# Projection of the last pairs: products 1 and 2 of the next pair issued among the last three products of a pair, in alternating PSUM banks

## Chip, cores and metric

One core of one Trainium2 chip. The metric is the device time of one execution in microseconds (us); before and after are compared by the median of several runs. The profile is of one execution, with a span that is a little shorter than its time.

## What is computed

```python
X = np.fft.rfft(x, axis=1)                    # x: 8 x 3136 x 256
y = np.fft.irfft(X * F, n=3136, axis=1)       # F: a complex filter, 1569 x 256
t = y.reshape(25088, 256)                     # tokens
h = t @ w_in                                  # 256 -> 1024
sm = softmax(h, axis=-1)
solu = h * sm
ln = (solu - mean(solu)) / np.sqrt(var(solu) + 1e-6) * g_ln
out = ln @ w_out                              # 1024 -> 256
```

## The kernel before

The Fourier filter is done as two short transforms by matrix products (49 x 64 points), one batch element after the other. Its results land in `y`, and tokens are taken from there in **blocks** of 128; there are 196 blocks, and two blocks make a **pair** (98 pairs, 0 to 97). The filter of later batch elements runs beside the token work of earlier ones; its last product (L353) and copy (L356) end at 1447.4 us of the span, and then only token work is left.

The order of all instructions on every engine is written out by hand: `step(k)` for k = 0 to 204 issues, for block k, what each engine does next, and each engine runs its own list in that order. A pair j = k // 2 takes two steps, an even and an odd one. Within a step several pairs are in flight at different depths:

- **Hidden products** (`product`, L680): `t @ w_in` of a pair of blocks is done by Strassen's scheme in Winograd's form, with seven products instead of eight. Their PSUM banks are m0 and m2 of the pool `ps_m`, and one from another pool. ScalarE keeps some copies (L690), VectorE finishes the halves of h and the row maximum (L701, L704). This is done for k < 196.
- **exp and normalizing**: two steps later ScalarE takes exp of h with a row sum (L712); VectorE makes the reciprocal of the sum (L723, L725) and solu (L728); ScalarE squares it for the variance (L730).
- **Turning**: three steps later VectorE transposes solu in 32 x 32 pieces (L738), and SyncE's queue regroups it with eight DMAs for a pair (`regroup`, L750): four write the buffer `solu_t0`, four `solu_t1`. Each of the two exists twice, so that the DMAs for pair p must wait until the last reader of pair p - 2 is done: for `solu_t1` that is product 4 of pair p - 2. For every second pair SyncE also writes and reads back the deviations (L758, L764: `rs_t`).
- **Sums for the projection** (`project_sums`, L658, GpSimd): four sums of the regrouped blocks, two in an odd step and two in the following even one.
- **Projection** (`project`, L792): `ln @ w_out` for pair p, again seven products, each of four 128 x 128 matmuls in float32, which the profile shows as 8 records. In the odd step the order is 1, 2, 6, 7, in the even step after it 5, 3, 4. Products 1, 6, 5, 3 go one after the other into one bank, 2, 7, 4 into the other; the banks are o0 and o1 of the pool `ps_o`, one each. 6, 5 and 3 are added on top of what their bank holds, 7 starts the other one anew and 4 adds to it; before each of 6, 5 and 3 ScalarE takes a scaled copy of the bank as it stands (`keep_out`, L804). VectorE finishes the four quarters of the output (`finish_out`: L811 adds a kept copy, L809 only scales). `store_out` (L819) stores the pair with two DMAs of SyncE's queue.

Nine steps lie between the first hidden product of a pair and its last projection (`LAG`). So the steps k = 196 to 204 have no hidden products any more: they project pairs 93 (second half), 94, 95, 96 and 97. This is the tail, the last 45 us of the span. In it the lists by engine are, before the change:

- TensorE: 5, 3, 4 of 93; 1, 2, 6, 7, 5, 3, 4 of 94; the same of 95, 96 and 97.
- SyncE: regroup 95 and store 93; regroup 96 first half, L758, regroup 96 second half, store 94; L764; regroup 97, store 95; store 96; store 97.
- ScalarE: with the copies of 5(93) come exp of block 194, square of 194, exp of 195, copy of 1(94), square of 195, copies of 6(94) and 5(94), and then the three copies of each pair.
- VectorE: normalizing of block 194, finish of 93, turn of 194, first finish of 94, normalizing of 195, turn of 195, and then the finishes.

The projection's first product of the next pair starts a new sum in o0, so it must wait until VectorE has read the last pair's sum there (L809); the second does the same in o1 (L811).

## Time and profile before

| what | us |
|---|---|
| median of 5 runs | 1682.4 |
| these runs, lowest and highest | 1678.14, 1689.17 |
| the profiled execution | 1687.0 |
| its span | 1685.2 |
| granted TensorE clock, mean over the span | 0.987 |

Engines: PE is TensorE (PEld its weight loads), DVE VectorE, ACT ScalarE, POOL GpSimd, SP SyncE; a q behind the name is its queue, issuing DMAs. A row of the timeline has the start, the length in us, the engine, the line of the kernel, the operation, output <- input, the number of records that were merged, and in brackets the idle time before it with the one that ended it. A row of the chain of waits has the start, the length and what the end of the kernel hung on at that time. A row of the windows has the stretch, its length, the busy us (and records) of PE, PEld, DVE, ACT and POOL, the granted TensorE clock as a share of full speed, the busy share of the DMA engines, and GB/s.

### The profile page before, as it was taken

The numbers are of one execution on the slowest core, as the hardware profiler recorded it, in microseconds if no ns is written. First come the engines' busy times: TensorE is split into PE (matmuls) and PEld (weight loads), VectorE is DVE, ScalarE is ACT, GpSimd is POOL, SyncE is SP. The second block draws the span as 40 slices with busy tenths as digits, with TensorE's granted clock in tenths as the row PEclk, the third lists the DMA queues.
The fourth block names the chain that finished last, engine by engine and source line by source line (L and its number), as shares of the span: only waits on it lengthen the run. The fifth ranks groups of instructions, "written<-read, shape, count | busy, mean of one in ns | idle before, by whom it ended". The sixth has DMA issues, their size and how long they took to land.

```text
span 1685.2 us, 31072 instructions
## 1 busy us (share of the span) xinstructions
PE 1602.5 (95%) x10022; PEld 1097.2 (65%) x10022; DVE 1262.9 (75%) x2619; ACT 937.9 (56%) x1730; POOL 1125.2 (67%) x1268
## 2 busy tenths in 40 slices
PE   5898899999999999999999999999999999999997
PEld 1353357756766676667766676667776777777776
DVE  1676887687777877887778878788778766777773
ACT  2154455556565556656565665556565666655551
POOL 4444786577667766787568866787566766676674
PEclk8999999999999999999999999999999999999999
DMA  9986868776787667865787668766776444444443
GB/s 258 258 272 207 252 175 224 212 212 171 196 231 212 190 181 215 246 184 150 206 238 205 175 154 231 228 178 170 199 207 170 114 125 124 100 108 106 109 111 96
DMA packets 375957, 311.72 MB, mean 185 GB/s; under 512 B 61514, under 2 KB 341571, under 8 KB 375795
## 3 DMA queue, kind: packets, MB, share of 16 engines
q1 hardware_dynamic: 306260, 169.81, 38.4%
q0 software_dynamic: 32640, 101.65, 20.4%
q10 hardware_dynamic: 36896, 38.28, 8.1%
q8 instruction: 81, 1.33, 0.3%
q14 instruction: 80, 0.66, 0.1%
HBM read 124.83 MB, written 81.50 MB: 122 GB/s over the span
## 4 chain that ended last, share of the span: by engine, by line
PE 67%; DMA 16%; DVE 7%; POOL 3%; SPq 3%; issue 3%; ACT 2%; ACTq 0%; DVEq 0%; POOLq 0%
PE m L680 27%; PE o L792 26%; DMA solu_t<-turn 7%; PE py L353 5%; PE pa L260 2%; SPq L750 2%; DMA out_dram<-ot 2%; PE pb L292 2%; PE pc L292 2%; DMA t<-d 2%; DVE h L728 2%; PE pa L217 1%; DVE turn L738 1%; DMA x<-in_x_dram 1%; POOL u L658 1%
## 5 line engine op out<-in xcount | busy, mean ns | idle before, releaser
L730 ACT ACTIVATE e<-h,nmu 128x1024 f32<-128x1024 f32 x196 | 225.3, 1150 | 366.8 <-DVE h L728 365.1
L792 PEld LDWEIGHTS o<-w_out_sb,solu_t 128*128 128x128 f32 x3136 | 380.9, 192 | 59.9 <-issue 40.7
L792 PE MATMUL o<-w_out_sb,solu_t 128*128 128x128 f32 x3136 | 401.2, 276 | 10.8 <-DVE rsum L723 7.5
L680 PE MATMUL m<-w_in_sb,s 128*128 128x512 f32 x784 | 403.0, 605 | 6.5 <-ACT h L690 4.6
L792 PEld LDWEIGHTS o<-w_out_sb,u 128*128 128x128 f32 x2352 | 306.0, 192 | 146.3 <-issue 112.6
L658 POOL TENSOR_TENSOR u<-solu_t 128x512 f32<-128x512 f32 x98 | 145.8, 1487 | 306.9 <-DMA solu_t<-turn 173.0
L680 PE MATMUL m<-w_in_sb,y 128*128 128x512 f32 x588 | 313.2, 616 | 15.1 <-DVE nmax L704 7.9
L792 PE MATMUL o<-w_out_sb,u 128*128 128x128 f32 x2352 | 313.7, 276 | 5.3 <-ACT ot L804 4.7
L728 DVE SCALAR_TENSOR_TENSOR h<-e,rsum,h 128x1024 f32<-128x1024 f32 x196 | 291.1, 1485 | 6.9
L811 DVE SCALAR_TENSOR_TENSOR ot<-o,rs_t,ot 128x128 f32<-128x128 f32 x294 | 102.4, 348 | 201.3 <-ACT ot L804 166.1
L690 ACT COPY h<-m 128x512 f32<-128x512 f32 x294 | 173.2, 589 | 131.9 <-PE m L680 114.3
L738 DVE STREAM_TRANSPOSE turn<-h 128x1024 f32<-128x1024 f32 x196 | 242.3, 1236 | 0.8
L712 ACT ACTIVATE e<-h,nmax 128x1024 f32<-128x1024 f32 x196 | 226.1, 1154 | 0.0
L658 POOL TENSOR_TENSOR u<-solu_t,u 128x512 f32<-128x512 f32 x98 | 143.5, 1464 | 86.3 <-PE o L792 82.3
L704 DVE CUSTOM_DVE_ANT_0 h<-m,h 128x512 f32<-128x512 f32 x196 | 133.1, 679 | 82.3 <-ACT h L690 60.7
L680 PEld LDWEIGHTS m<-w_in_sb,y 128*128 128x128 f32 x588 | 94.9, 191 | 123.0 <-DVE nmax L704 63.2
L680 PEld LDWEIGHTS m<-w_in_sb,s 128*128 128x128 f32 x784 | 124.2, 191 | 68.8 <-issue 45.4
L356 ACT COPY y<-py 128x392 f32<-128x392 f32 x128 | 109.3, 854 | 106.2 <-PE py L353 104.5
L353 PEld LDWEIGHTS py<-wi_t,t 100*128 100x128 f32 x1024 | 132.3, 192 | 54.9 <-issue 42.6
L658 POOL TENSOR_TENSOR solu_t<-solu_t,solu_t 128x512 f32<-128x512 f32 x98 | 152.4, 1555 | 7.7
L658 POOL TENSOR_TENSOR u<-u,solu_t 128x512 f32<-128x512 f32 x98 | 134.4, 1372 | 0.7
L353 PE MATMUL py<-wi_t,t 100*128 100x98 f32 x1024 | 131.6, 273 | 1.7 <-DMA t<-d 1.3
(108 smaller groups left out, 1984.2 us busy)
## 6 DMA issues: line engine op xcount, KB each, us to landing
solu_t<-turn SPq DMA_DIRECT2D x784, 128.0 KB
out_dram<-ot SPq DMA_DIRECT2D x196, 128.0 KB
t<-d POOLq DMA_DIRECT2D x56, 400.0 KB, 5.0
d<-x POOLq DMA_DIRECT2D x100, 200.0 KB, 5.4
f<-f_dram POOLq DMA_DIRECT2D x39, 512.0 KB, 6.9
d<-g POOLq DMA_DIRECT2D x39, 512.0 KB, 5.2
t<-d ACTq DMA_DIRECT2D x36, 512.0 KB
x<-in_x_dram SPq DMA_DIRECT2D x112, 98.0 KB
```

The costliest lines, as they stand in the source:

```text
L353: nc.tensor.matmul(out=psv[:, i:2 * NCH - i:2 * NCH - 1 - 2 * i, :], lhsT=t4s[e, ch][:, i, cb * P:cb * P + P], rhs=wi_t, start=True, stop= ...
L356: evac(out=y[:, cb, t0:t0 + S].rearrange("p (r m j) -> p m j r", m=N2 // NCH, j=NCH)[:, ch:last + 1 - ch:last - 2 * ch], in_=psv.rearrange ...
L658: nc.gpsimd.tensor_tensor(out=out, in0=in0, in1=in1, op=op)
L680: nc.tensor.matmul(out=ms[j, bank], lhsT=lhsT, rhs=w_in_sb[:, w, :], start=m in (1, 2, 7), stop=True, skip_group_check=True)
L690: nc.scalar.copy(out=h_half(k, i), in_=ms[j, 0])
L704: nc.vector.tensor_tensor_reduce(out=h_half(k, i), in0=ms[j, bank], in1=h_half(*kept), scale=1.0, scalar=sofar, op0=ALU.add, op1=ALU.min, ...
L712: nc.scalar.activation(out=e, in_=hs[k], func=AFT.Exp, bias=nmaxs.pop(k)[:, 1:2], scale=-1.0, accum_out=esum)
L728: nc.vector.scalar_tensor_tensor(out=solu, in0=e, scalar=rsum, in1=solu, op0=ALU.mult, op1=ALU.mult, accum_out=nmu)
L730: nc.scalar.activation(out=e, in_=solu, func=AFT.Square, bias=nmu, scale=-float(DFF), accum_out=variances[g][:, i:i + 1])
L738: nc.vector.transpose(out=turns[g][:, :, i, :], in_=solus.pop(k).rearrange("p (f j) -> p f j", j=32))
L792: nc.tensor.matmul(out=pos[p, bank], lhsT=lhs[:, f, :], rhs=w[:, f, :], start=f == 0 and m in (1, 2, 7), stop=True, skip_group_check=True)
L811: nc.vector.scalar_tensor_tensor(out=ot, in0=pos[p, bank], scalar=rs, in1=out_half(p, *kept)[0], op0=ALU.mult, op1=ALU.add)
```

## The change

In the even steps of the tail (no hidden products left), product 1 of the next pair and its scaled copy are issued after product 5 of the pair, and product 2 of the next pair after product 3. The order becomes 5(p), 1(p+1), 3(p), 2(p+1), 4(p), 6(p+1), 7(p+1). Since the sums of both pairs are then open at the same time, pairs 94 and 96 use the banks m0 and m2, which no hidden product uses any longer; 95 and 97 stay in o0 and o1. The copy of product 1 moves on ScalarE with it. The order on VectorE, GpSimd and SyncE is the same as before.

```diff
@@ project
         if m in (1, 2):
-            pos[p, bank] = ps_o.tile([P, DFF // 2], FP32, name=f"o{m}_{p}", tag=f"o{bank}")[:, 0:P]
+
+            space, tag = (ps_m, "m") if p > begun_late and (p - begun_late) % 2 else (ps_o, "o")
+            pos[p, bank] = space.tile([P, DFF // 2], FP32, name=f"o{m}_{p}", tag=f"{tag}{2 * bank if tag == 'm' else bank}")[:, 0:P]
@@ before step
+    begun_late = pairs - (LAG + 1) // 2
@@ step
         hid, proj = k < blocks, p is not None
+
+        along = not hid and not odd and p + 1 < pairs
@@ even step
+            if along:
+                project(p + 1, 1)
+                keep_out(p + 1, 0, (0, 0))
             if proj:
                 project(p, 3)
+            if along:
+                project(p + 1, 2)
+            if proj:
                 project(p, 4)
@@ odd step
             if proj:
-                project(p, 1)
-                keep_out(p, 0, (0, 0))
-                project(p, 2)
+                if p <= begun_late:
+                    project(p, 1)
+                    keep_out(p, 0, (0, 0))
+                    project(p, 2)
                 finish_out(p, 0, 0, (0, 0), 1)
```

`begun_late` is 98 - 5 = 93. The condition `along` holds in steps 196, 198, 200 and 202.

## The prediction

> I write 3(94) for product 3 of the projection of pair 94. Five pairs, 93 to 97, are projected after the last hidden product; only there does the change act. The page, the times and the waits before that point stay: instruction for instruction, the order on every engine is the same up to step 196.

> **What bounds the kernel now.** First the page.

> ```profile
> span 1685.2 us, 31072 instructions
> PE 1602.5 (95%) x10022; PEld 1097.2 (65%) x10022; DVE 1262.9 (75%) x2619; ACT 937.9 (56%) x1730; POOL 1125.2 (67%) x1268
> ```

> TensorE is busy 95% of the span, so one would guess that waits taken from it are worth their length. But these waits are all behind 1640 us, and a stage is read from itself. So next the chain of waits of the last 45 us.

> ```profile
> 1652.81 1.17 PE o L792 x8
> ...
> 1654.52 2.04 PE o L792 x16
> 1656.55 0.02 issue
> 1656.57 0.59 SPq L750
> ...
> 1667.41 2.43 DMA solu_t<-turn
> ...
> 1673.88 2.96 PE o L792 x24
> ```

> From 1656.57 to 1667.41 the chain is not on TensorE at all: it is SyncE's queue, issuing DMAs one by one. Then one landing, GpSimd's sums, and TensorE again for the last pair. The queue itself, from the timeline:

> ```profile
> 1639.34 7.59 SPq L750 DMA_DIRECT2D solu_t<-turn  x8
> 1647.03 1.30 SPq L819 DMA_DIRECT2D out_dram<-ot  x2
> 1652.60 2.68 SPq L750 DMA_DIRECT2D solu_t<-turn  x4
> 1655.38 0.55 SPq L758 DMA_DIRECT2D rows<-rs  x1
> 1656.57 2.59 SPq L750 DMA_DIRECT2D solu_t<-turn  x4
> 1659.26 1.30 SPq L819 DMA_DIRECT2D out_dram<-ot  x2
> 1660.67 1.87 SPq L764 DMA_DIRECT2D rs_t<-rows  x4
> 1662.65 5.37 SPq L750 DMA_DIRECT2D solu_t<-turn  x8
> ```

> Read it so: from 1656.57 to 1668.02 there is no gap over 0.11 us; the queue is full. What starts it is the second regrouping of pair 96, which overwrites the buffer that 4(94) reads last: 4(94) ends at 1656.54, the DMA starts at 1656.57. Everything after (the loads of pair 97 landing at 1669.84, its sums, 6(97) at 1673.88, the last store) hangs on that by fixed lengths. **So the end moves by what the end of 4(94) moves**, whatever TensorE gains elsewhere.

> **The change, part by part.** Nothing is added or taken away: 8 products (1 and 2 of pairs 94 to 97) and 4 scaled copies (L804) move; no DMA does. The order 5, 3, 4 of pair p, then 1, 2 of p+1, becomes 5, 1(p+1), 3, 2(p+1), 4. One product is 8 records at a pitch of 0.111 (24 records, last end after 2.84 us, in the row at 1655.48): 0.89 us.

> 1. Waits removed. 3(p) waited 0.55 us for the copy of 5(p) on ScalarE, for pairs 93 to 96; now 1(p+1) fills it: 4 x 0.55 = 2.2. 1(94) waited 1.93 us for VectorE's finish of pair 93's bank; with banks m0 and m2, which VectorE last read by 1640.2 (L704), it needn't. On TensorE alone that is 4.1 us.

> 2. The chain ahead of 5(94). ScalarE's copy of 1(94) and VectorE's finish behind it stand between ScalarE's exp of block 195 and VectorE's L723 now: exp ends 1648.55, copy to 1648.81, finish 1648.88 to 1649.23, L728 starts 1649.52. After, the copy runs at 1643.3, where ScalarE waits 2.74 us for L728 of block 194 anyway, and L723 follows exp directly. By the same pair in the block before (L723 1643.32, L728 1643.71) L728 starts at 1648.58 + 0.39 = 1648.97: 0.55 earlier. It took 1.66 because GpSimd's sum ran from 1648.81; that sum waits for DMAs behind 4(93), which ends 0.99 later now (1(94) and 2(94), 1.78, are ahead of it; the wait that they fill is 0.79 from start to start: 5(93) at 1640.60 would pass on at 1641.59, 3(93) starts at 1642.31 and loses 0.07 more at its start), so it starts at 1649.8 and L728 takes its undisturbed 1.28: another 0.38. Square and copy follow, and 5(94) starts at 1652.81 - 0.93 = 1651.88.

> 3. From 5(94) to the end of 4(94). Before: 1652.81 to 1656.54 = 3.73 (5, the wait, 3, 4). After five products without a wait: 0.10 + 5 x 0.89 + 0.17 = 4.72, end at 1656.60. **The two inserted products (1.78) cost 0.99 more than the wait that they fill, and part 2 gives 0.93 back: +0.06 us.** The first DMAs of pair 96 start earlier (the turn of block 195 ends 1651.5), but they fill the queue only until 1655.0, so 4(94) stays the last releaser.

> 4. The clock. TensorE's work moves away from 1646 to 1652: after 6(94), ending 1646.2, only 7(94) is left (it waits for VectorE's finish of 2(94), behind the turn that ends 1647.6; 1.05 us long), then nothing until 1651.88. What such a gap does is in the windows of before:

> ```profile
> 1644.26:1647.67 3.41, 1.48 (x13) 1.41 (x13) 3.36 (x5) 1.60 (x3) 0.59 (x1) 1.00 0.46 118
> 1647.67:1651.09 3.42, 3.26 (x16) 2.99 (x16) 2.14 (x4) 1.13 (x3) 2.20 (x2) 0.50 0.36 101
> 1651.09:1654.50 3.41, 2.06 (x16) 1.69 (x16) 1.42 (x4) 1.86 (x4) 3.04 (x4) 1.00 0.17 47
> ```

> Second number: TensorE's busy us; the 0.50 is the granted clock. 1.48 us of 3.41 busy were followed by 3.41 us at half clock (6(94) took 2.04 for 8 records instead of 1.16); 2.06 were not. That cold stretch is free today: 1, 2, 6 and 7(94) ran in it, with ScalarE and VectorE as the chain. After, 5.7 us hold 1.05 us of work, so a cold stretch follows nearly wherever the 3.41 us cells fall, and it lies on 5(94) to 4(94). Price: at least nothing (cells that fall so that it ends before 1651.9), at most 5 x 0.88 = 4.4 (all five cold, 2.04 against 1.16 each). A cold cell wholly over critical work costs half its 3.41 us, 1.7. If the idle cell starts at 1646.2, the cold one is 1649.6 to 1653.0 and overlaps by 1.1; if at 1650, by 3.4; and often the next cell is too empty as well. I take **+1.5**, near the row's one cold cell.

> [...]

> 5. Behind 4(94). New order, new queueing: 3(96) now stands behind 1(97), which waits for the loads of pair 97; they land 2.43 after an issue ending about 1665.4, 1667.8, and 5(96) occupies TensorE to 1668.9. Cover 1.1 us. ScalarE's copy of 1(96) still waits for rs_t at 1665.45 and that of 1(97) for a store's landing (1673.17); behind them stand only copies that need 6(96) and 6(97), which wait for them anyway. GpSimd and SyncE keep their order. SyncE loses a wait for TensorE at the first regroupings of 96 and 97, which were not late. TensorE has 14 products (12.5 us) between 1656.6 and 6(97) at 1673.9: 4.8 us of slack. Cost 0.

> Sum: +0.06 + 1.5 = **+1.6 us**: span 1685.2 to 1686.8, profiled execution 1687.0 to 1688.6. That execution lies 4.6 above the median, 1682.4; the difference, put on the median, gives **1684.0**.

> **Rivals.**
> - Smaller, or slightly gained (about 1682.4). L728 of block 194 takes 2.24 us because GpSimd's sum got in first:

> ```profile
> 1643.59 1.27 POOL L658 TENSOR_TENSOR u<-solu_t,u 128x512 f32<-128x512 f32 x1 [0.92 <-PE o L792]
> ...
> 1643.71 2.22 DVE L728 SCALAR_TENSOR_TENSOR h<-e,rsum,h 128x1024 f32<-128x1024 f32 x1
> ```

> That sum waits for 3(93), which ends 0.10 later after the change: 1643.69 against 1643.71. If VectorE wins, L728 takes 1.28 and all of the chain is 0.94 earlier: -0.9 warm, +0.6 cold. Against it: at 1575.5 VectorE was 0.03 us ahead (1575.52 and 1575.55) and still took 2.37, while 0.08 ahead at 1637.67 it took 1.28. With POOL first and the clock warm it is +0.06.
> - TensorE is the bound after all: then the 4.1 us of part 1 are kept: 1678.3. For it, the 95%; against it, the full queue.
> - Slower: TensorE stays at half clock through the whole tail, and becomes the bound. 24 products from 5(94) to the end are 21.4 us warm, 42.7 cold. Beyond the first cell, each cold cell costs 1.7; the slack takes 4.8, so from the third further cell on TensorE decides, and it needs about 8 of the 10 cells to cost 8.4 us; all give 1684 + 15 = 1699. For it, the row above; against it, a cold stretch doubles TensorE's busy time, and the next cell was warm (3.26 busy, then 1.00).
> - The change doesn't do what it says: TensorE still waits for VectorE, because the m banks are held. Against it, L704 done by 1640.2. Then 4(94) is later by the wait too, 1.9: 1686.

> **How the numbers follow.** Likeliest: +0.7 to +4.4, at +1.6, chance 0.53. Smaller or slightly gained: 0.33. TensorE bound: 0.06. Slower by over 8: 0.03. The waits stay: 0.05. All but one lie within 0.5% (8.4 us, about what a measurement of this kernel can tell). The range must hold the scatter of the runs too, 1678.14 to 1689.17 around 1682.4, larger than any term: 1678 to 1690. Faster by over 0.5% 0.02 (scatter alone), slower 0.04 (the cold tail and scatter).

> **What would show it.** Right: TensorE never waits for VectorE's L809 (now L811) before 1(94); 5(94) starts about 0.9 earlier against the first L750 of pair 95; a 0.50 clock lies on 5(94) to 4(94); regrouping 96 starts as 4(94) ends; the queue stays full to the last regrouping. Wrong: the queue starts by another releaser, TensorE is busy through from 6(95) to the end, or the store at the end waits for more than 4(97).

## The result and the profile after

| what | before | after |
|---|---|---|
| median of all timed runs, us | 1684.76 (79 runs) | 1687.93 (44 runs) |
| lowest and highest, us | 1674.88, 1695.76 | 1681.44, 1695.51 |
| the profiled execution, us | 1687.0 | 1688.69 |
| its span, us | 1685.2 | 1686.9 |
| granted TensorE clock, mean over the span | 0.987 | 0.983 |

The ratio of after to before is 1.0021, with a 95% interval of 1.0011 to 1.003. On a median of 1684.76 that is +3.5 us (1.9 to 5.1): under the 0.5% named in the prediction, but the interval leaves out zero. The changed kernel is slightly slower. The sum forecast was +1.6, the range of the likeliest case +0.7 to +4.4.

The head of the page shows the same engines, 95% and 75% as before, and helps no further:

```profile
span 1686.9 us, 31067 instructions
PE 1604.2 (95%) x10022; PEld 1098.7 (65%) x10022; DVE 1261.3 (75%) x2619; ACT 938.3 (56%) x1730; POOL 1120.3 (66%) x1268
```

The spans differ by 1.7, close to the forecast of 1.6, but that is an accident. 5(93), the first product of the tail, starts at 1640.60 in the profile of before and at 1637.56 in that of after: a difference of 3.04 in favour of the changed kernel, in work that the change does not touch. Over the 14 profiles of this study it starts anywhere from 1631.4 to 1642.2, so that runs scatter ahead of the tail by more than any term of the sum. What can be compared is **the tail, from the start of 5(93) to the end of the span: 44.62 before, 49.35 after, +4.73.** All times below that are called "in the tail" count from the start of 5(93).

TensorE's timeline of the changed kernel, around pair 94 (the rows from 1644.97 are 7(94), 5(94), 1(95), 3(94), and 2(95) with 4(94)) and at 6(97):

```profile
1644.97 1.16 PE L794 MATMUL o<-w_out_sb,solu_t 128*128 128x128 f32 x8 [1.79 <-DVE ot L813]
1648.98 2.08 PE L794 MATMUL o<-w_out_sb,u 128*128 128x128 f32 x8 [2.85 <-ACT ot L806]
1650.85 1.92 PE L794 MATMUL o<-w_out_sb,solu_t 128*128 128x128 f32 x8
1652.55 1.36 PE L794 MATMUL o<-w_out_sb,u 128*128 128x128 f32 x8
1653.76 1.95 PE L794 MATMUL o<-w_out_sb,solu_t 128*128 128x128 f32 x16
...
1674.14 2.04 PE L794 MATMUL o<-w_out_sb,u 128*128 128x128 f32 x8 [2.57 <-POOL u L658]
```

The new order is there: five products without an idle time in brackets. But the first two take 2.08 and 1.92 for 8 records, where 7(94) took 1.16. The windows of the same kernel, over the six cells of the clock that matter:

```profile
1642.95:1646.36 3.41, 1.40 (x11) 1.01 (x9) 2.60 (x9) 2.48 (x4) 0.00 (x0) 1.00 0.61 153
1646.36:1649.77 3.41, 0.79 (x3) 0.80 (x4) 2.22 (x3) 1.50 (x3) 2.79 (x2) 0.50 0.25 76
1649.77:1653.19 3.42, 3.42 (x18) 3.42 (x17) 0.35 (x1) 0.74 (x2) 2.49 (x4) 0.50 0.64 158
1653.19:1656.60 3.41, 3.41 (x31) 3.41 (x31) 0.96 (x3) 0.00 (x0) 1.27 (x1) 1.00 0.02 2
...
1670.26:1673.67 3.41, 1.31 (x12) 1.12 (x10) 0.35 (x1) 0.04 (x1) 3.33 (x3) 1.00 0.27 89
1673.67:1677.08 3.41, 2.94 (x14) 2.97 (x15) 0.35 (x1) 0.69 (x2) 1.64 (x2) 0.50 0.17 60
```

Two cells in a row hold only 1.40 and 0.79 us of TensorE's work, and each is followed by a cell at 0.50: the half clock lasts from 1646.36 to 1653.19, over most of the five products. Then it returns where nobody had looked for it: 1.31 us of work ahead of 6(97), and 0.50 on the products of the last pair. SyncE's queue in between:

```profile
1648.68 2.68 SPq L750 DMA_DIRECT2D solu_t<-turn  x4
1651.46 0.55 SPq L758 DMA_DIRECT2D rows<-rs  x1
1655.74 2.58 SPq L750 DMA_DIRECT2D solu_t<-turn  x4
1658.42 1.30 SPq L821 DMA_DIRECT2D out_dram<-ot  x2
1659.83 1.87 SPq L764 DMA_DIRECT2D rs_t<-rows  x4
1661.80 6.46 SPq L750 DMA_DIRECT2D solu_t<-turn  x8
```

As before, the queue is released by the end of 4(94) (1655.70; the DMA starts at 1655.74) and is full from there on. But its last group takes 6.46 where it took 5.37: the chain of waits shows its DMAs one by one.

```profile
1661.80 0.67 SPq L750
...
1665.87 0.62 SPq L750
...
1666.53 3.52 DMA solu_t<-turn
...
1674.14 4.33 PE o L794 x24
```

Each takes 0.58 to 0.67, but the last, at 1666.53, kept the queue for 1.72 (the group ends 6.46 after 1661.80, at 1668.26).

So the tail's +4.73 is made up like this. 5(94) starts at 11.41 in the tail and not at 12.21: -0.80. The five products have two more in them: +0.99. They run partly at half clock (5(94) starts 11.41, 4(94) ends 18.14: 6.73, where five products without a wait take 4.72): +2.0. One slow issue in the queue: +1.1. 6(97) to the end of 4(97) takes 6.89, not 5.52, as it begins at half clock: +1.4. Sum +4.7. **The order alone costs about 0.2; the half clock costs 3.4, in two places, and the slow issue 1.1.** That the slow issue comes of the change isn't said by this profile. For the last of these terms, this is 6(97) in the profile of before, with a shorter wait and at full clock:

```profile
1673.88 1.16 PE L792 MATMUL o<-w_out_sb,u 128*128 128x128 f32 x8 [0.64 <-POOL u L658]
```

### The profile page after: what moved, and what is told of

The parts are those of the page before. It is cut to its first block, busy times and chain, and to the rows that moved or that the text cites. A ratio compares the mean times of both kernels' runs of the same rounds, so it can differ in the third digit from the quotient of the medians.

```text
span 1686.9 us, 31067 instructions
## 1 busy us (share of the span) xinstructions
PE 1604.2 (95%) x10022; PEld 1098.7 (65%) x10022; DVE 1261.3 (75%) x2619; ACT 938.3 (56%) x1730; POOL 1120.3 (66%) x1268
## 3 DMA queue, kind: packets, MB, share of 16 engines
q10 hardware_dynamic: 36896, 38.28, 7.9%
q8 instruction: 81, 1.33, 0.3%
## 4 chain that ended last, share of the span: by engine, by line
PE 67%; DMA 16%; DVE 7%; SPq 3%; issue 2%; POOL 2%; ACT 1%; ACTq 0%; DVEq 0%; POOLq 0%
PE m L680 27%; PE o L794 26%; DMA solu_t<-turn 8%; PE py L353 5%; PE pa L260 2%; PE pb L292 2%; DMA t<-d 2%; PE pc L292 2%; DMA x<-in_x_dram 2%; SPq L750 2%; DVE h L728 2%; DVE turn L738 1%; DMA f<-in_filt_r_dram 1%; PE idler L492 1%; DVE ot L813 1%
## 5 line engine op out<-in xcount | busy, mean ns | idle before, releaser
L658 POOL TENSOR_TENSOR u<-solu_t 128x512 f32<-128x512 f32 x98 | 147.0, 1500 | 316.9 <-DMA solu_t<-turn 157.5
L728 DVE SCALAR_TENSOR_TENSOR h<-e,rsum,h 128x1024 f32<-128x1024 f32 x196 | 286.7, 1463 | 6.9
L658 POOL TENSOR_TENSOR u<-solu_t,u 128x512 f32<-128x512 f32 x98 | 142.8, 1458 | 86.9 <-PE o L794 82.8
L704 DVE CUSTOM_DVE_ANT_0 h<-m,h 128x512 f32<-128x512 f32 x196 | 133.2, 679 | 82.7 <-ACT h L690 60.7
L658 POOL TENSOR_TENSOR solu_t<-solu_t,solu_t 128x512 f32<-128x512 f32 x98 | 150.5, 1535 | 7.7
L658 POOL TENSOR_TENSOR u<-u,solu_t 128x512 f32<-128x512 f32 x98 | 136.2, 1390 | 0.7
```

What stands on the lines that cost most here:

```text
L658: nc.gpsimd.tensor_tensor(out=out, in0=in0, in1=in1, op=op)
L704: nc.vector.tensor_tensor_reduce(out=h_half(k, i), in0=ms[j, bank], in1=h_half(*kept), scale=1.0, scalar=sofar, op0=ALU.add, op1=ALU.min, ...
L728: nc.vector.scalar_tensor_tensor(out=solu, in0=e, scalar=rsum, in1=solu, op0=ALU.mult, op1=ALU.mult, accum_out=nmu)
```

## The experiments

The theory: as the prediction's part 4 has it, the cost is the half clock, which follows on a cell of 3.41 us with too little work (1.40, 0.79 and 1.31 us in the rows above). New in it is that a second such cell arises ahead of 6(97). The rivals: the slow issue belongs to the change and not to chance; TensorE's own work, two products more ahead of 4(94), is what costs; and the queue hides a gain that is there.

One table first, to which all of the experiments refer. The times are us in the tail, of one profile each; "regroup 96" is the start of the second half of its issue, "last regroup" the first issue of that of pair 97 to the end of its last; "half clock" is the stretches in the tail with the clock at 0.50, without the very end.

| kernel | 5(94) starts | 4(94) ends | regroup 96 | last regroup | 6(97) starts | 4(97) ends | tail | half clock |
|---|---|---|---|---|---|---|---|---|
| before | 12.21 | 15.94 | 15.97 | 22.05 to 27.42 | 33.28 | 38.80 | 44.62 | 7.07-10.48 |
| e9, before again | 13.56 | 19.94 | 19.97 | 26.04 to 32.32 | 38.38 | 43.87 | 49.76 | 6.28-9.69, 13.11-19.93 |
| e10, before, third | 12.23 | 15.96 | 16.00 | 22.07 to 28.22 | 34.38 | 39.87 | 45.78 | none |
| after | 11.41 | 18.14 | 18.18 | 24.24 to 30.70 | 36.58 | 43.47 | 49.35 | 8.80-15.63, 36.11-39.52 |
| e1, after again | 11.41 | 18.18 | 18.21 | 24.26 to 30.95 | 36.78 | 44.93 | 50.82 | 8.87-15.70, 36.18-43.01 |
| e2, after filled | 11.41 | 16.14 | 16.18 | 23.06 to 28.41 | 34.34 | 39.82 | 45.70 | none |
| e3, before filled | 12.21 | 17.48 | 17.51 | 23.58 to 29.82 | 36.02 | 41.51 | 47.42 | 13.74-17.15 |
| e4, own buffer | 11.42 | 19.03 | 14.97 | 22.11 to 28.34 | 34.36 | 41.48 | 47.35 | 10.67-17.49, 34.56-37.97 |
| e5, 2(p+1) behind | 11.42 | 17.95 | 17.98 | 24.06 to 29.41 | 35.28 | 40.77 | 46.68 | 10.28-17.11, 27.35-30.76 |
| e6, first pair only | 11.41 | 17.53 | 17.56 | 23.64 to 29.97 | 35.89 | 41.38 | 47.27 | 11.72-18.54 |
| e7, before, queue freed | 13.61 | 19.99 | 17.24 | 22.08 to 27.41 | 35.75 | 41.16 | 47.08 | 6.34-9.76, 13.17-20.00 |
| e8, after, queue freed | 11.41 | 17.49 | 14.97 | 20.71 to 26.71 | 32.63 | 38.15 | 44.04 | 10.85-14.26 |
| e11, after, relieved | 11.42 | 16.15 | 14.98 | 21.27 to 23.84 | 32.81 | 38.30 | 44.27 | 25.85-29.26 |
| e12, before, relieved | 12.22 | 15.96 | 20.92 | 27.59 to 30.16 | 38.28 | 43.69 | 49.62 | 22.24-25.65 |

From the end of 4(97) to the end of the span it is 5.8 to 5.97 in all of them.

### e1: the changed kernel once more

No edit. 

> The changed kernel once more. Tail means the time from the start of 5(93) to the end of the span: 44.6 us before, 49.3 in the profile after. Main theory (the queue waits for 4(94), half-clock stretches of 3.41 us do the rest): 5(94) at 11.4 and the second regrouping of pair 96 at the end of 4(94) again; where the half-clock stretches lie changes with the run, so the tail is 44.8 (none on critical work) to 49. Rival (a slow DMA issue, 1.72 us in the profile after, belongs to the change): the same 1.1 us in the last regrouping again. Time: 1 to 5 us above before.

Measured: tail 50.82; 1687.28 us, ratio 1.0021 (0.9999 to 1.0043). The tail is 1.8 over the expected range's upper end. Both half-clock stretches are there again, and the one on pair 97 is a cell longer. TensorE's timeline of e1 at 6(97), 7(97) and 5(97):

```profile
1673.79 2.07 PE L794 MATMUL o<-w_out_sb,u 128*128 128x128 f32 x8 [3.02 <-POOL u L658]
1675.65 1.92 PE L794 MATMUL o<-w_out_sb,solu_t 128*128 128x128 f32 x8
1677.36 1.92 PE L794 MATMUL o<-w_out_sb,u 128*128 128x128 f32 x8
```

Three products at about 2 us each: 6(97) to the end of 4(97) is 8.15, against 5.52 before, +2.6. The last regrouping has a slow issue again (1.96). Two profiles with one can still be chance; e3, e9 and e10 settle that.

### e2: the changed kernel, with the gaps filled

```diff
+    def fill(n):
+        ps = ps_b[0].tile([P, 512], FP32, name="fill", tag="b")
+        for _ in range(n):
+            nc.tensor.matmul(out=ps, lhsT=w_out_sb[:, 0, 0, :], rhs=w_in_sb[:, 0, :], start=True, stop=True)
@@ odd step, around products 6 and 7
+                if p in (96, 97):
+                    fill(2)
                 project(p, 6)
+                if p == 94:
+                    fill(1)
                 project(p, 7)
+                if p == 94:
+                    fill(2)
```

The added products go to a bank that nothing reads; the computation is whole. 

> The changed kernel with 128x512 products of no use (0.86 us each) in TensorE's gaps: one between 6(94) and 7(94), two between 7(94) and 5(94), two each before 6(96) and 6(97); all fit into the gaps of the profile after (1.79, 2.85, 3.05, 2.57). Main theory: no half clock between 5(93) and the last product; of the 4.7 us that the tail grew, the 2.0 on 5(94) to 4(94) and the 1.4 on 6(97) and 7(97) go: tail 44.8 to 46.0, time 0 to 1.5 above before. Rival (the clock is not what costs; the inserted products or the banks do): tail 48 to 49, time 3 to 5 above before.

Measured: no half clock anywhere in the tail; the five products take 4.73 (11.41 to 16.14), and 6(97) to 4(97) 5.48. The windows of e2 over the stretch after 7(94), and its timeline, where L903 is the fill:

```profile
1648.40:1651.80 3.40, 2.28 (x10) 1.14 (x9) 2.25 (x3) 1.50 (x3) 2.37 (x2) 1.00 0.33 91
```

```profile
1648.04 1.88 PE L903 MATMUL fill<-w_in_sb,w_out_sb 128*128 128x512 f32 x4
1651.05 1.16 PE L794 MATMUL o<-w_out_sb,u 128*128 128x128 f32 x8 [1.12 <-ACT ot L806]
1652.04 1.06 PE L794 MATMUL o<-w_out_sb,solu_t 128*128 128x128 f32 x8
...
1671.25 1.88 PE L903 MATMUL fill<-w_in_sb,w_out_sb 128*128 128x512 f32 x4
1673.97 1.13 PE L794 MATMUL o<-w_out_sb,u 128*128 128x128 f32 x8 [0.84 <-POOL u L658]
```

5(94), in the row at 1651.05, has 1.16 where it had 2.08, and 6(97) 1.13 where it had 2.04; the waits for ScalarE and GpSimd are still there, only shorter by the fill. The tail is 45.70, with one slow issue on the path (an L764 that took 1.25, so 0.8 more than usual): 44.9 without it, against 44.62 before. **Useless work on TensorE takes 3.4 us from the tail (2.0 up to 4(94), 1.4 from 6(97) on; the whole tail is 3.7 shorter, as its slow issue is also a shorter one), so what cost was the clock and not the number of products.** The time, 1684.91, has a ratio to before of 1.0008 (0.9991 to 1.0025), so it isn't told from before. Beside e1, the changed kernel timed along with it, the medians differ by 2.4 (95% interval -0.1 to 6.9, by resampling the 12 runs of each) and the means, 1684.9 and 1688.5, by 3.6 (1.2 to 6.1): the time comes down with the fill too, by an amount that is only roughly known.

### e3: the kernel before, filled in the same way

```diff
@@ odd step
+                if p == 94:
+                    fill(2)
                 project(p, 1)
```

(`fill` is that of e2.)

> The kernel before with two such products in the gap ahead of 1(94) (1.93 us). Main theory: the half clock that stood at 7.1 to 10.5 after 5(93) goes, but lay beside ScalarE's and VectorE's chain, so the tail stays at 44.6 within 0.5 and the time within 1 of before. Rival (half clock costs in the kernel before too): tail about 1 to 1.5 shorter.

Measured: tail 47.42, not 44.6; 1685.71 us, ratio 1.0001 (0.9981 to 1.0022). The fill took away the first cold stretch and a later one came. The windows of e3:

```profile
1644.06:1647.47 3.41, 1.20 (x9) 0.97 (x8) 1.48 (x3) 1.83 (x4) 3.03 (x4) 1.00 0.16 47
1647.47:1650.88 3.41, 3.23 (x15) 3.27 (x16) 0.70 (x2) 0.03 (x1) 1.82 (x2) 0.50 0.55 133
```

The cell that 5(94) falls into had 1.20 us of work, and the next one, with 3 and 4(94) in it, ran at half: 4(94) ended at 17.48, 1.5 late. So the old order has the same weak place, and in the profile of before the half clock happened to fall ahead of it. A slow issue (1.50) stands in the last regrouping of this old order too: the rival of e1, that it belongs to the change, falls.

### e4: a buffer of its own for the second half of pair 96

```diff
@@ regroup
-        st = upool.tile([P, KF, P], FP32, name=f"solu_t_{p}_{i}", tag=f"solu_t{i}")
+        if p == 96 and i == 1:
+            st = pools["r"].tile([P, NCH, C], FP32, name=f"solu_t_{p}_{i}", tag="r").rearrange(
+                "p n (h c) -> p (n h) c", c=P)
+        else:
+            st = upool.tile([P, KF, P], FP32, name=f"solu_t_{p}_{i}", tag=f"solu_t{i}")
```

> The changed kernel with a buffer of its own (one of the row buffers, idle by then) for the second half of regrouped pair 96, so that these four DMAs need not wait for 4(94). Main theory: they are issued at 14.5 after 5(93) instead of 18.2; the next entry in the queue, the store of pair 94, then waits for the last finish after 4(94), so the queue gains 4 issues less the wait, about 2.3 us: tail 2 shorter than the changed kernel at the same clock, 45 to 47. Rival (TensorE is the bound): tail as the changed kernel's.

Measured: SyncE's queue in e4.

```profile
1652.13 3.29 SPq L754 DMA_DIRECT2D solu_t<-turn  x4
1655.52 1.67 SPq L825 DMA_DIRECT2D out_dram<-ot  x2
1657.30 1.86 SPq L768 DMA_DIRECT2D rs_t<-rows  x4
1659.27 6.22 SPq L754 DMA_DIRECT2D solu_t<-turn  x8
```

The regrouping of 96 no longer waits for 4(94) (14.97 in the tail, where 14.5 was expected); the store of pair 94 behind it does, and the last regrouping begins at 22.11 and not at 24.24: 2.1 earlier, 2.3 expected. The hold of 4(94) on the queue is this buffer, then. The rest of the tail (47.35, just over the expected 45 to 47) has the half clock twice again and a slow issue in each of the two regroupings (1.33 and 1.49). Time 1683.56, ratio to before 0.9992 (0.9973 to 1.0011).

### e5: product 2 of the next pair behind 4(p)

```diff
@@ even step
-            if along:
-                project(p + 1, 2)
             if proj:
                 project(p, 4)
+            if along:
+                project(p + 1, 2)
```

> The changed kernel with product 2 of the next pair behind product 4 instead of ahead of it: 5, 1(p+1), 3, 4, 2(p+1). Main theory: 4(94) ends one product earlier (0.89 at full clock, up to 1.8 at half), and the queue with it, the end by as much: tail 47.5 or less where the clock is low on 5(94) to 4(94), 43.9 where it is full; 1 to 2 us less time than the changed kernel. Rival (TensorE is the bound): nothing changes, since TensorE does the same products without a gap.

Measured: 4(94) ended at 17.95, only 0.2 earlier than after, with one product less ahead of it: here the half clock lasted from 10.28 to 17.11 in the tail and so covered 5, 1, 3 and part of 4(94). The tail is 46.68, as there is neither a second cold stretch on pair 97 (the second one lies earlier, at 27.35, and 6(97) waits for nothing) nor a slow issue in the last regrouping; 1685.23 us, ratio 1.0013 (0.9991 to 1.0035). It speaks against TensorE's amount of work as the price, but weakly: the clock's phase was another.

### e6: the new order for the first pair only

```diff
-        along = not hid and not odd and p + 1 < pairs
+        along = not hid and not odd and p == begun_late
@@ odd step
-                if p <= begun_late:
+                if p != begun_late + 1:
```

> Only the first of the four steps changed: 1 and 2 of pair 94 among the products of 93; 95 to 97 in the old order (96 still in the m banks). Main theory: 5(94) at about 11.4 as in the changed kernel, but nothing is inserted ahead of 4(94): it ends 3.7 later at full clock, 15.2, or up to 17.3 where the half clock of the emptied 6 us lies on 5, 3 and 4(94); tail 43.9 to 46.2. No half clock ahead of 6(97), since the old order keeps TensorE busy there. Rival (inserted products do no harm, the emptied gap does all): tail as the changed kernel, 48 to 49.

Measured: 4(94) ends at 17.53, 2.4 later than at full clock (11.41 and 3.73), although no product is inserted between 5(94) and 4(94): the half clock lies on nearly all of the three. In the changed kernel it ended at 18.14, so here the emptied gap does most of the harm and the two inserted products 0.6 of it. And 6(97) to 4(97) takes 5.49, with no half clock, as expected. The tail, 47.27, is 1.1 over the expected range's upper end, and 1.0 of that is a slow issue. 1686.7 us, ratio 0.9999 (0.9976 to 1.0022). No half clock on pair 97 agrees with the other profiles: it stands there in after, e1 and e4, where the products of pairs 96 and 97 are moved, and in none of the seven profiles that have these pairs in the old order.

### e7 and e8: the queue freed, in the old order and in the new

The second half of 96 and both halves of 97 get buffers of their own, and so do, in a common one, the output tiles of 96 and 97 (four buffers of the "r" pool, free in the tail). Pair 97 is regrouped right behind pair 96 and the deviations, two steps earlier and ahead of the stores. e7 has this edit on the kernel before, e8 on the one after; the diff shows its main parts.

```diff
@@ regroup
-        st = upool.tile([P, KF, P], FP32, name=f"solu_t_{p}_{i}", tag=f"solu_t{i}")
+        if (p, i) in ((96, 1), (97, 0), (97, 1)):
+            st = pools["r"].tile([P, NCH, C], FP32, name=f"solu_t_{p}_{i}", tag="r").rearrange(
+                "p n (h c) -> p (n h) c", c=P)
+        else:
+            st = upool.tile([P, KF, P], FP32, name=f"solu_t_{p}_{i}", tag=f"solu_t{i}")
@@ even step, behind regroup(j - 3, 1)
+            if j - 3 == pairs - 2:
+                regroup_deviations((j - 3) // 2)
+                regroup(j - 2, 0)
+                regroup(j - 2, 1)
```

> The kernel before with the queue relieved: the second half of 96 and all of 97 go to row buffers that are idle by then, and pair 97 is regrouped right after 96 and the deviations, ahead of the stores; the last two output tiles lie in such a buffer too. Main theory: the queue no longer sets the end; TensorE does, with 4(94) at 15.9 and three pairs of 7.0 each behind it: last product at 37 instead of 38.8, tail 42.8. Rival (something else than the queue sets the end): tail 44.6.

> The same relief in the changed kernel. Main theory: with the queue out of the way the order of the change is worth its waits: 4(94) at 16 (full clock) to 18.2, then 19 products at 0.89 and the end of 97: last product at 34 to 36, tail 39.7 to 41.7, less than the kernel before with the same relief (42.8). So the same edit gains 1 to 3 us here and loses 3 where the queue is full. Rival (the change is bad for TensorE itself): above 42.8.

Measured: tail 47.08 (e7) and 44.04 (e8); 1684.62 and 1684.3 us, ratios 0.9999 (0.9979 to 1.0018) and 0.9997 (0.9973 to 1.0021). Both are later than expected, e7 by the clock (a first stretch delays 5(94) to 13.61, a second lies on 5 to 4(94) wholly: 4(94) ends at 19.99), e8 by the clock ahead of 4(94) (17.49), slow issues in the queue (1.51 and 1.32) and a wait of 1.85 of 6(97) for the sums. e8's tail lies where its rival put it, above 42.8. But from the end of 4(94) on, e7 does what was said. TensorE's timeline of e7 around 6(97), the row at 1667.18:

```profile
1664.50 2.84 PE L796 MATMUL o<-w_out_sb,solu_t 128*128 128x128 f32 x24
1667.18 1.06 PE L796 MATMUL o<-w_out_sb,u 128*128 128x128 f32 x8
```

No bracket: 6(97) waits for nothing. The last three pairs take 21.17, or 7.06 each (7.0 expected); before, the same stretch took 22.86. With the queue out of the way TensorE is the bound in the old order, and there the change's saved waits should count. In e8 the stretch is 20.66, so 0.5 shorter; the other 2.5 of their difference is the clock on 4(94). Whether the change gains with a free queue is therefore not settled.

### e9 and e10: the kernel before, twice more

No edit, one run each. 

> The kernel before once more, for its tail. Main theory: its gaps ahead of 1(94) (1.93 us), 5(94) and 3(94) (0.82 and 0.55) can also empty a 3.41 us cell so that the half clock falls on 5(94) to 4(94), as it did with the filled gap (tail 47.4); how often decides the mean difference. Tail 44.6 to 47.5, with at most one such stretch on work that the queue or the end waits for. Rival (the kernel before never pays for the clock): 44.6 within 0.5, plus 1.1 for each slow DMA issue.

> The kernel before a third time, the same expectation: tail 44.6 to 47.5 by the clock and slow DMA issues; 44.6 within 0.5, plus 1.1 for each slow issue, by the rival.

Measured: tails 49.76 and 45.78; 1683.3 and 1688.78 us. The one with the longer tail is the faster run, since it reached the tail earlier: a single time says nothing here. e9's tail is 2.3 over the expected range's upper end. e9 is the kernel before with the price that the prediction had for the kernel after. Its windows:

```profile
1634.63:1638.04 3.41, 1.48 (x13) 1.29 (x13) 3.34 (x7) 0.84 (x1) 1.27 (x1) 1.00 0.31 78
...
1641.46:1644.87 3.41, 1.43 (x13) 1.24 (x11) 3.38 (x3) 1.09 (x2) 1.13 (x1) 1.00 0.10 36
1644.87:1648.28 3.41, 2.41 (x9) 2.14 (x10) 0.45 (x2) 0.77 (x4) 2.45 (x3) 0.50 0.42 105
1648.28:1651.70 3.42, 3.42 (x17) 3.42 (x17) 0.35 (x1) 0.00 (x0) 1.27 (x1) 0.50 0.22 52
```

And its products, first 1 and 2(94), then 5(94) and 3(94):

```profile
1637.43 3.25 PE L792 MATMUL o<-w_out_sb,solu_t 128*128 128x128 f32 x16 [1.93 <-DVE ot L809]
...
1645.33 2.08 PE L792 MATMUL o<-w_out_sb,u 128*128 128x128 f32 x8 [2.43 <-ACT ot L804]
...
1647.95 2.04 PE L792 MATMUL o<-w_out_sb,u 128*128 128x128 f32 x8 [0.55 <-ACT ot L804]
```

The cells lie 0.8 earlier against the work than in the first profile of before (6.28 in the tail, not 7.07). So the cold stretch takes 1(94) with it, whose copy the chain ahead of 5(94) needs (5(94) starts 1.35 later), and a second one lies on 5, 3 and 4(94): 4.0 us in all to the end of 4(94). In e10 there is none at all. Both have a slow issue in the last regrouping (1.54 and 1.40).

### e11 and e12: queue freed, one regrouping on ScalarE's queue, and gaps filled

To e8 and e7 is added that the second half of 97 is issued by ScalarE, ahead of that of 96, and fills: in e11 one after 6(94) and two after 7(94), in e12 two before 1(94) and one after 7(94).

```diff
-    def regroup(p, i):
+    def regroup(p, i, dma=nc.sync.dma_start):
@@ even step
+            if j - 3 == pairs - 2:
+                regroup(j - 2, 1, nc.scalar.dma_start)
             if 0 <= j - 3 < pairs - 1:
                 regroup(j - 3, 1)
```

> The changed kernel with the queue relieved further (the second half of 97 issued from ScalarE's queue right after the first half of 96, the first half of 97 on SyncE's queue right after 96 and the deviations) and products of no use in the two gaps around 7(94). Main theory: loads of 97 land at about 25 after 5(93), so TensorE is the bound: 4(94) at 16.2, then 19 products at 0.89 and the end of pair 97: last product at 34, tail 39.8 to 41; time 3 to 6 us below before. Rival (a further bound, such as GpSimd's sums or the landing of stores, near the queue): tail 43 to 45.

> The same in the old order of products, with products of no use ahead of 1(94) and 5(94). Main theory: 4(94) at 15.9, then three pairs of 7.0: last product at 37, tail 42.8 to 44, so 2 to 3 us longer than the changed kernel with the same relief: with a free queue the change gains what its part 1 promised for three pairs, less what the two inserted products cost. Rival: no difference, 43 to 45 in both.

Measured: e11 tail 44.27, 1683.93 us, ratio 0.9988 (0.9972 to 1.0005); e12 tail 49.62, 1688.85 us, 1.0016 (0.9998 to 1.0034). In e11 4(94) ends at 16.15 as expected, but other bounds take over. The queue and TensorE of e11, where the regrouping of 96 takes 3.98 with a wait of 1.5 inside, and 6(96) waits for GpSimd:

```profile
1653.15 3.98 SPq L754 DMA_DIRECT2D solu_t<-turn  x4
```

```profile
1663.00 1.16 PE L798 MATMUL o<-w_out_sb,u 128*128 128x128 f32 x8 [2.35 <-POOL u L658]
```

On the wait of 6(96) follows a half-clock stretch, which lies on 7(96) and 5(96) (25.85 to 29.26, about 1.7 us lost). These two make up 4.0 of the 4.3 us by which the last product ends later than the theory's 34 (at 38.30). The tail is in the rival's range, 43 to 45, and not in the theory's. e12 is spoiled as a comparison. Its queue:

```profile
1641.92 10.19 SPq L827 DMA_DIRECT2D out_dram<-ot  x2
1652.28 2.68 SPq L754 DMA_DIRECT2D solu_t<-turn  x4
```

A store of pair 93 that otherwise takes 1.30 held SyncE's queue for 10.19 and put the regrouping of 96 at 20.92 (its first half at 16.80, the second behind it). SyncE's waits in e12 name what its second DMA waited for:

```profile
SPq L827 <- DMA solu_t<-turn: 8.9, 1, 8.9
```

That is the landing of a regrouping, of which the store needs nothing. In the trace this DMA waits for, and then counts, the same semaphore as the first of the four DMAs that ScalarE issues for pair 97: that one landed at 15.97 in the tail, and the store's DMA started at 16.03. The wait in e11 is of the same kind (landing at 17.01, start at 17.03). So the experiments' own edit made these waits, by completion semaphores that DMAs of the two queues share; a version without the sharing wasn't run. No version here is shown to be faster than the kernel before.

## Why the prediction was right, and where it was not

- **The waits that go (part 1): right.** TensorE waits no more for VectorE before 1(94), nor for the copy between 5 and 3. That this buys nothing by itself was right too: regroup 96 starts within 0.04 us of the end of 4(94) in every kernel of the table that leaves its buffer alone.
- **The chain ahead of 5(94) (part 2): right**, -0.80 for -0.93; 11.41 or 11.42 in all kernels with the new order. L728 of block 195 took 1.28 as forecast. In the block before, GpSimd came first again (1640.65 against 1640.67) and L728 took 2.33, so the small gain of the first rival didn't come.
- **5(94) to 4(94) (part 3): right.** At full clock (e2) 4(94) ended at 16.14 in the tail, against 15.94: +0.2 for +0.06.
- **The clock (part 4): the mechanism right, the comparison wrong.** The half clock cost +2.0 up to the end of 4(94) in both profiles of the changed kernel, for +1.5: two empty cells came in a row (1.40 and 0.79 us of work in the profile of after), not one. No idle time of TensorE in any tail was over 3.31 us (2.85 ahead of 5(94) here), so none was as long as a cell; cells with 0.57 to 1.49 us of work were enough. What failed is "That cold stretch is free today": the kernel before pays 4.0 up to 4(94) in e9, and with two products of no use in its gap it pays 1.5 in e3. One profile had shown the cells at a phase where they cost it nothing. Taken over the profiles without fills, the price up to 4(94) is 0, 4.0, 0 and 4.0 in the old order (before, e9, e10, e7) and 2.0, 2.0, 2.9 and 1.4 in the new one (after, e1, e4, e8, against the 16.14 of e2): 2.0 and 2.1 in the mean. So these profiles don't show the +1.5 as a difference between the two orders at all.
- **"Behind 4(94)" (part 5), "Cost 0": wrong.** The slack was counted rightly, but not where it lies. With 1, 2 and 3 issued early, TensorE's idle time gathers in single gaps, 3.05 us ahead of 6(96) and 2.57 (e1: 3.02) ahead of 6(97), where before it was 0.64. The second gap empties a cell, and the half clock falls on 6(97) and after, on the path: +1.4 after, +2.6 in e1, +1.6 in e4, 0 in e2, where the gap is filled, and 0 in every profile of the old order. The prediction looked for cells emptied by the change only ahead of 5(94). The slow issue has a part in the gap: after, e1 and e4 all have one in the last regrouping. In the old order it widens the gap too (1.68 to 2.20 in e9, e10, e3 and e6), but there the cell kept at least 1.61 us of work and no half clock followed. What the new order does at this place with neither a slow issue nor a fill nor another half clock just ahead is not on record.
- **The slow issue, +1.1, was not in the sum**, and rightly so: it is in old and new orders alike (in the last regrouping of e9, e10, e3 and e6 among the seven profiles with the old order there, and of after, e1, e4 and e8 among the other seven).
- **The number: inside the range, in part by luck.** +3.5 lies in +0.7 to +4.4, and the likeliest case named the right cause. But the term that made up nearly all of the sum is not shown to differ between the orders, and a term that was put at 0 is the one that does in these profiles.

The tails then fit the times, as far as few profiles can: 46.7 us is the mean of the three tails of before (44.62, 49.76, 45.78) and 50.1 that of the two of after, a difference of 3.4 beside 3.5 (1.9 to 5.1) timed. The agreement rests on five profiles. The granted clock of all the runs points the same way: it is 0.9844 in the mean over the 44 runs of after, 0.9866 over the 89 runs of before that were timed with the experiments, and 0.9860 over the 12 of e2. The first two make about 7.5 us more at half clock in a run of the changed kernel; half of that, 3.7, is an estimate of what it costs if all of it lies on the path. What is shown is that the half clock costs the tail 3.4 us in the profile of after (against e2). That it makes up all of the timed difference is likely, not shown, since e2's time is not told from that of before and lies only roughly 2 to 4 us under that of the changed kernel. Open: what the change would give with the queue out of the way.

## What to carry to other kernels

A product that is moved to fill a small wait takes its work from somewhere else: look at where the idle time gathers afterwards, cell by cell, and at what runs in the next cell (here 2.57 us ahead of 6(97), in a cell that was left with 1.31 us of work, and 1.4 us lost behind it). Before a wait is taken away, find the resource that the next stage really starts from, here a buffer that SyncE's queue waits for; if the last reader of it doesn't get earlier, the time saved on TensorE is idle time. And when a term is smaller than the scatter of runs, compare the stretch it acts in, over several profiles of both kernels, as one profile of before can be a lucky one (the three tails here: 44.62, 49.76 and 45.78 us).
